# Top-k attention and Fourier mixing on one Trainium2 core: the scores of a pair's first tile queued last in TensorE's step

## The chip, the cores and the metric

The kernel runs on one core of a Trainium2 chip. The core has a TensorE for matmuls (PE in the profile; its weight loads are shown as PEld), a VectorE (DVE), a ScalarE (ACT), a GpSimd (POOL) and a SyncE (SP), which issues the DMAs here. Each engine works through its own list of instructions in order; the lists are tied together by semaphores. The metric is the device time of one execution in microseconds.

## The reference

Two stages follow one another. In the first, 8 batches of 8 heads attend over 576 tokens with 64 channels a head, and only the 32 largest scores of a row are kept. The second takes the heads side by side as 512 channels, adds the real part of a two-dimensional Fourier transform over tokens and channels, normalises, and applies an MLP of width 2048 with a residual.

```python
scores = scale * np.matmul(q, k.transpose(0, 1, 3, 2))
kth = np.partition(scores, -top_k, axis=-1)[..., -top_k:-top_k + 1]
scores = np.where(scores >= kth, scores, -1000000000.0)
attn = np.exp(scores - np.max(scores, axis=-1, keepdims=True))
attn = attn / (np.sum(attn, axis=-1, keepdims=True) + 1e-09)
x = np.matmul(attn, v)                  # heads are then put side by side: (8, 576, 512)
...
mixed = np.real(np.fft.fft(np.fft.fft(x, axis=1), axis=2)).astype(np.float32)
u = x + mixed
un = (u - np.mean(u, -1, keepdims=True)) / np.sqrt(var + 1e-06)
out = u + np.maximum(un @ w_ch1, 0.0) @ w_ch2
```

All inputs and outputs are float32.

## The kernel before

**Tiles and pairs.** Two heads of a batch make a *pair*; there are 32 pairs, four to a batch. The 576 rows of queries are cut into four tiles of 128 rows and one of 64. A pair is worked through as nine *items*, in the order of `IN_PAIR`: tile 0 for each head, tile 1 for each head, the 64-row tile for both heads at once, tile 2 and tile 3 for each head. So item 9p is pair p's first tile, first head.

**The steps.** The main loop runs one *step* for each item number i, and in a step all engines get work of several items, a few items apart, so that none waits for another:

- `scores(j, ...)` for item j = i + 3: TensorE multiplies the queries (qT) by the first 512 keys (kT) for both heads of the tile (L401, tiles `sp`), and by the 64 last keys of both (kt, L371, `sp_t`). ScalarE copies the results from PSUM to the tile S in SBUF (L404 and L375; for the 64-row tile L386 on TensorE and L393 on ScalarE).
- `top_ops`: VectorE finds the 32 largest of a row, eight at a time (L425, L427); it finishes item i and begins item i + 1.
- `bounds` (POOL, L434, tile `nt`), `mask` (ScalarE L448, then POOL's subtraction L451) and `expo` (ScalarE L459) turn the scores of item i - 1 into unnormalised probabilities P.
- P must be transposed for the product with v. In the first batch and in pairs 7 and 31 TensorE does this (`transposes`, L527 to L545). In the others, those for which `pair_by_dma` holds (pairs 4 to 30 without 7), it goes by DMA: ScalarE splits P into two planes of 16-bit words (`plane`, L472, item i - 2), a DMA writes them to DRAM (L485, L488), and a transposing DMA (`turn`, L506, item i - 3) reads them back as PT. All three are issued in SP's order.
- `attend` (TensorE L564) multiplies PT by v, and `to_tokens` (TensorE L604, tile `tpx`) brings the result back to token rows, which VectorE normalises (L608).
- `prep` transposes the q and k of the next pair on TensorE (L308, tiles `tpq`, `tpk`); ScalarE copies them to qT and kT (L316, L318) and to kt (L322). k's turn is in step 9p + 5, q's in step 9p.
- `some` fills TensorE with *units* of the MLP of the batch before: `hidden` (hp, L966; ScalarE applies the ReLU at L970), `back` (cp, L993 and L1032), and `fast` (cv, cw, cz, L1163, a product with seven instead of eight sub-products, whose sums POOL makes at L1108).
- Once in a batch the Fourier transform of the batch before stands in a few steps: POOL folds x (L651 to L719), TensorE transforms over tokens (`dft_tokens`, yp, L755), ScalarE copies y (L786 to L798), TensorE transforms over channels (`dft_channels`, mp, L812 and L816), ScalarE copies us (L833), POOL adds it to x (L839), and VectorE takes the statistics (L844).

**What sets the order.** The order on every engine is written out by the program: the loop body appends TensorE's work of a step to the list `fixed` and then calls the entries one after the other; a call records all instructions of that piece of work on all engines, so a piece's ScalarE copies stand in ScalarE's list where the piece was called. After each entry, `some` adds MLP units up to that entry's share of the room that the step has by the planner's costs (`step_us`, `fixed_cost`, `level`). Before the first entry the step records `turn`, `mask` of item i - 1 and `plane` of item i - 2. After the entry with number `n_mask` = 0 come pieces put off from earlier (`act`, `out_next`). After the last entry before the transposes comes `expo` of item i - 1; in the pairs by DMA that is the end of the list.

The scores of a tile are the first entry of `fixed`. For a tile whose two heads are separate items and whose pair goes by DMA, both parts are one entry, at the first head's step. For a pair's first tile this is step 9p - 3, that is the step right after the one in which `prep` made the kT of that pair.

Of the kernel before, what the change touches and what calls it, by code (L numbers as in the profile page):

```python
# [73 lines left out]
def kernel(  # L74
# [55 lines left out]
    def bank(shape, name, hold=False):  # L130
        n = banks_free.pop(0)
        t = ps_m.tile(shape, F32, name=name, tag=f"m{n}", bufs=1)
        if not hold:
            banks_free.append(n)
            return t
        return t, lambda: banks_free.append(n)
# [157 lines left out]
    def prep(n, pair, blocks=((0, NF), (NF, NC))):  # L294

        if pair >= NPAIR:
            return 0.0
        src, got_of = nat[n, pair], qT_of if n == "q" else kT_of
        if pair not in got_of:
            got_of[pair] = attp.tile(  # L300
                [P, S if n == "q" else NF * P], F32, name=f"{n}T_{pair}", tag=f"{n}T",
                bufs=2 if n == "q" else 1
            )
        t_sb = got_of[pair]
        for c0, c1 in blocks:
            tp = ps_t.tile([P, 4, P], F32, name=f"tp{n}_{pair}_{c0}", tag="tp")
            for c in range(c0, c1):
                nc.tensor.transpose(  # L308
                    tp[:, c - c0, :], src[:, c, :, :].rearrange("p h d -> p (h d)"), ident
                )  # L310
            if c0 < NF:
                dst, got = t_sb[:, c0 * P:c1 * P], tp.rearrange("p a c -> p (a c)")[:, 0:(c1 - c0) * P]
            else:
                dst, got = t_sb[:, NF * P:], tp[:, 0, 0:TAIL]
            if n == "q":
                nc.scalar.mul(out=dst, in_=got, mul=scale)  # L316
            elif c0 < NF:
                nc.scalar.copy(out=dst, in_=got)  # L318
            else:
                for e in range(2):  # L320
                    r = slice(D * e, D * (e + 1))
                    nc.scalar.copy(out=kt_t[r, TAIL * e:TAIL * (e + 1)], in_=tp[r, 0, 0:TAIL])  # L322
        return 0.7
# [3 lines left out]
    PER_PAIR = len(IN_PAIR)  # L327
    PER_BATCH = NPB * PER_PAIR
# [3 lines left out]
    N = len(items)  # L332

    def scores(i, part):

        if not 0 <= i < N:
            return 0.0
        pair, t, e = items[i]  # L340
        qT, kT = qT_of[pair], kT_of[pair]
        rows = ROWS[t]
        if part == 0:
            for n in range(1 if e is None else 2):
                Ssb[i + n] = attp.tile([P, S], F32, name=f"S_{i + n}", tag="S", bufs=6)
        q_cols = slice(P * t, P * t + rows)


        plain = (slice(0, NF * P), slice(NF * P, S))
        tails_first = (slice(TAIL, S), slice(0, TAIL))  # L350
        if e is None:
            to = [
                (Ssb[i], slice(TAIL * h, TAIL * (h + 1)), *(tails_first if h and by_dma(i) else plain))
                for h in range(2)
            ]
        else:
            to = [
                (Ssb[i], slice(0, P), *plain),
                (Ssb[i + 1], slice(0, P), *tails_first),
            ]  # L360
        if part == 1:

            copy = nc.scalar.copy if i else nc.vector.tensor_copy
            shape, name = [P, NF * P], f"sp_{i}_t"
            if by_dma(i):
                sp = ps_t.tile(shape, F32, name=name, tag="tp")
            else:
                sp = ps_s.tile(shape, F32, name=name, tag="sp") if i else bank(shape, name)

            q_end = P * t + rows  # L370
            nc.tensor.matmul(  # L371
                sp[:, 0:P], lhsT=qT[:, q_end - P:q_end], rhs=kt_t, start=True, stop=True
            )
            for h, (s_t, r, _, tails) in enumerate(to):
                copy(out=s_t[r, tails], in_=sp[P - rows:P, TAIL * h:TAIL * (h + 1)])  # L375
            return 0.3
        if e is None and i >= PER_BATCH:

            half = NF * P // 2
            sps = [  # L380
                ps_s.tile([P, NF * P], F32, name=f"sp_{i}_{h}", tag="sp") for h in range(2)
            ]
            for g in range(2):
                for h in range(2):
                    hd = slice(D * h, D * (h + 1))
                    nc.tensor.matmul(  # L386
                        sps[h][TAIL * g:TAIL * (g + 1), 0:half],
                        lhsT=qT[hd, q_cols], rhs=kT[hd, half * g:half * (g + 1)],
                        start=True, stop=True,
                    )  # L390
            for h, (s_t, r, keys, _) in enumerate(to):
                for g in range(2):
                    nc.scalar.copy(  # L393
                        out=s_t[r, keys][:, half * g:half * (g + 1)],
                        in_=sps[h][TAIL * g:TAIL * (g + 1), 0:half],
                    )
            return 0.6
        for h, (s_t, r, keys, _) in enumerate(to):
            hd = slice(D * h, D * (h + 1))
            sp = ps_s.tile([P, NF * P], F32, name=f"sp_{i}_{h}", tag="sp")  # L400
            nc.tensor.matmul(  # L401
                sp[r], lhsT=qT[hd, q_cols], rhs=kT[hd, :], start=True, stop=True
            )
            nc.scalar.copy(out=s_t[r, keys], in_=sp[r])  # L404
        return 1.04
# [32 lines left out]
    def pair_by_dma(pair):  # L438

        return NPB <= pair < NPAIR - 1 and pair != 2 * NPB - 1  # L440

    def by_dma(i):
        return pair_by_dma(i // PER_PAIR)
# [999 lines left out]
    def chunk_at(i):  # L1443

        for tile in (i - 4, i - 3, i - 2):
            r = tile % PER_PAIR
            if PER_BATCH <= tile < N and r in (4, 8):
                if i - tile == (4 if by_dma(tile) else 2 if tile == 2 * PER_BATCH - 1 else 3):
                    return tile // PER_PAIR, r // 8
        return None, None  # L1450

    def fixed_cost(i):

        t = 0.55 if 0 <= i - 2 < N and not by_dma(i - 2) else 0.0
        if i + 3 < N:
            t += {0: 1.04, 1: 0.3, None: 0.9}[items[i + 3][2]]
            if by_dma(i + 3) and items[i + 3][2] is not None:
                t += -0.3 if items[i + 3][2] else 0.3
        ch = chunk_at(i)[1] if i > PER_BATCH + 3 else {4: 0, 8: 1}.get((i - 3) % PER_PAIR)
        t += 0.0 if ch is None else (CW[ch] / 115.0 + 0.14 * len(CHUNKS[ch]))  # L1460
        if i < N and i % PER_PAIR in (0, 5):
            t += 0.7
        return t + costs.get(i, 0.0)

    def level(i):

        steps = range(i, next((a for a in arrivals if a > i), i + PER_BATCH))
        rest, lev = sum(u[0] for u in queue + waiting), 0.0
        while lev < 6.4 and sum(max(0.0, lev - fixed_cost(s)) for s in steps) < rest:
            lev += 0.02  # L1470
        return lev

    def run(i, where):
        for fn in plan.pop((i, where), []):
            fn()
# [16 lines left out]
    while i < N + 5 or plan or queue or sums:  # L1492
# [11 lines left out]
        fixed, j = [], i + 3  # L1504
        e = items[j][2] if j < N else None
# [4 lines left out]
            preps.append(lambda: prep("q", pair_of + 1))  # L1510
        if i < N and i % PER_PAIR == 5:
            preps.append(lambda: prep("k", pair_of + 1))
        if e == 0 and by_dma(j):
            fixed.append(lambda: scores(j, 0) + scores(j, 1))
        elif e != 1:
            fixed.append(lambda: scores(j, 0))
        elif not by_dma(j):
            fixed.append(lambda: scores(j - 1, 1))
        else:
            fixed.append(lambda: 0.0)  # L1520
# [30 lines left out]
        if i in arrivals:  # L1551
            carry = min(carry, 0.0) if i > arrivals[0] else -5.0
            run(i, "units")
            step_us = level(i)
        room = step_us - carry - fixed_cost(i)
        cost, got = carry, 0.0
        turn(i - 3)
# [105 lines left out]
```

## Time and profile before

| | |
|---|---|
| median of three runs | 1877.12 us (1875.2 to 1878.28) |
| the profiled execution, its own time | 1876.57 us |
| its span, first to last instruction | 1874.8 us |
| mean granted TensorE clock | 0.955 |
| costliest group on TensorE | hp L966, 529.5 us, 2048 matmuls |
| costliest group on VectorE | L425, 626.5 us, 864 instructions |
| scores on TensorE, L401 | 170.7 us, 528 matmuls |
| transposing DMAs, L506 | 130, issued by SP |

The profile is one execution. A timeline line has the start in us from the span's beginning, the duration, the engine, the source line, the operation, tiles as out<-in, shapes and the number of instructions merged into the line; in brackets stands how long the engine was idle before it, and what ended that. A line of waits has the waiting group, what it waited for, the total in us, how many times, and the longest. A line of windows has the stretch and its length, then for each engine the busy time and the number of instructions, then the granted TensorE clock (1.00 is full speed), the busy share of the DMA engines, and GB/s. The slices on the page cut the span into 40 equal parts and give the busy tenths of each.

In TensorE's lines a float32 matmul appears as two records, so the two 512-key products of a tile are four records of L401.

### The profile page before, as it was taken

Reading aid. Unit: us, or ns where it says so; the run is one execution under the profiler, and the core shown is the slowest. Engines: PE = TensorE matmul, PEld = TensorE weight load, DVE = VectorE, ACT = ScalarE, POOL = GpSimd, SP = SyncE. Lnnn points to the kernel's source line nnn. Section 1 sums busy time; section 2 is a strip of 40 time slices with the busy share of each in tenths; the row PEclk is TensorE's granted clock in tenths of the full one; section 3 lists DMA queues with packets and bytes.
Section 4 is the critical chain, followed back from the end, with each engine's and each line's share of the span. In section 5 each row is a group of like instructions: output and inputs, shape, how many; then the busy total and the mean of one; then the engine's idle time right before and its main releaser. Section 6 shows DMA issues by size and latency. Waiting matters only on the chain.

```text
span 1874.8 us, 26903 instructions
## 1 busy us (share of the span) xinstructions
PE 1703.8 (91%) x8134; PEld 1086.4 (58%) x8134; DVE 1583.8 (84%) x3301; ACT 1295.0 (69%) x3104; POOL 912.5 (49%) x1278
## 2 busy tenths in 40 slices
PE   5566699789899899999999999989999999999999
PEld 3344465355466555666556565666567555677677
DVE  7999989888899999999999899899999899762110
ACT  6878659577788788877787678767787678652100
POOL 4768643454746266355545465255545364341012
PEclk7777799999999999999999999999999999999999
DMA  5333016661557755586466745694566645530132
GB/s 167 104 98 109 20 46 170 168 164 26 137 146 202 187 130 136 150 209 161 123 161 180 180 114 132 155 231 127 122 162 182 172 121 143 130 111 6 51 114 69
DMA packets 516576, 249.16 MB, mean 133 GB/s; under 512 B 398288, under 2 KB 506448, under 8 KB 516432
## 3 DMA queue, kind: packets, MB, share of 16 engines
q1 hardware_dynamic: 515664, 247.23, 50.9%
q8 instruction: 65, 1.06, 0.2%
q14 instruction: 79, 0.65, 0.1%
q10 hardware_dynamic: 768, 0.21, 0.0%
HBM read 93.63 MB, written 84.74 MB: 95 GB/s over the span
## 4 chain that ended last, share of the span: by engine, by line
PE 55%; DVE 13%; ACT 10%; POOL 10%; issue 6%; DMA 4%; SPq 2%; POOLq 0%; DVEq 0%; ACTq 0%
PE hp L966 22%; PE o L564 7%; DVE wk L427 6%; DVE m L425 6%; PE sp L401 4%; PE cp L993 4%; POOL wk L451 4%; PE cw L1163 3%; PE cv L1163 3%; PE cp L1032 3%; ACT wk L448 2%; POOL fg L651 2%; PE yp L755 2%; ACT wk L472 2%; PE sp_t L371 2%
## 5 line engine op out<-in xcount | busy, mean ns | idle before, releaser
L451 POOL TENSOR_TENSOR wk<-S,wk 128x576 f32<-128x576 f32 x288 | 408.1, 1417 | 549.8 <-ACT wk L448 533.9
L425 DVE MAX8 m<-wk 128x8 f32<-128x576 f32 x864 | 626.5, 749 | 6.2
L966 PE MATMUL hp<-unT,w 128*128 128x256 f32 (+1 forms) x2048 | 529.5, 411 | 5.2 <-ACT unT L884 2.7
L966 PEld LDWEIGHTS hp<-unT,w 128*128 128x128 f32 x2048 | 382.5, 192 | 116.5 <-issue 10.7
L427 DVE MATCH_REPLACE8 wk<-m,wk 128x576 f32<-128x576 f32 x576 | 427.4, 742 | 0.0
L472 ACT COPY wk<-S 128x576 uint16<-128x576 uint16 x468 | 289.1, 668 | 0.0
L448 ACT ACTIVATE wk<-S,nt 128x576 f32<-128x576 f32 x288 | 222.9, 774 | 85.4 <-POOL nt L434 84.5
L564 PE MATMUL o<-PT,v 128*64 128x256 f32 (+3 forms) x1440 | 204.8, 430 | 37.9 <-DMA PT<-planes 19.5
L993 PE MATMUL cp<-w,hT 128*128 128x512 f32 x512 | 236.4, 602 | 0.0
L425 DVE MAX8 m<-S 128x8 f32<-128x576 f32 x288 | 213.5, 741 | 7.8 <-ACT S L375 7.8
L459 ACT ACTIVATE S<-wk,nt 128x576 f32<-128x576 f32 x234 | 184.2, 787 | 48.3 <-POOL wk L451 47.2
L427 DVE MATCH_REPLACE8 wk<-m,S 128x576 f32<-128x576 f32 x288 | 213.5, 741 | 0.0
L970 ACT ACTIVATE hT<-hp 128x320 f32<-128x320 f32 (+1 forms) x256 | 103.9, 412 | 156.3 <-PE hp L966 155.2
L401 PE MATMUL sp<-kT,qT 64*128 64x512 f32 (+1 forms) x528 | 170.7, 676 | 24.2 <-ACT kT L318 9.4
L564 PEld LDWEIGHTS o<-PT,v 128*64 128x64 f32 x1440 | 117.9, 158 | 114.9 <-issue 37.0
L404 ACT COPY S<-sp 128x512 f32<-128x512 f32 (+1 forms) x264 | 141.6, 586 | 24.4 <-PE sp L401 23.3
L993 PEld LDWEIGHTS cp<-w,hT 128*128 128x128 f32 x512 | 93.4, 193 | 91.4 <-issue 91.0
L1108 POOL TENSOR_TENSOR hT<-hT 128x512 f32<-128x512 f32 x64 | 81.6, 1277 | 106.5 <-ACT hT L970 91.5
L434 POOL TENSOR_TENSOR nt<-m,cc 128x2 f32<-128x2 f32 x288 | 59.1, 205 | 126.2 <-DVE m L425 122.5
L371 PEld LDWEIGHTS sp_t<-kt,qT 128*128 128x128 f32 x320 | 51.3, 196 | 108.9 <-issue 70.0
L1163 PE MATMUL cw<-w,hT 128*128 128x256 f32 x448 | 105.0, 381 | 1.5 <-POOL hT L1108 0.9
L527 PE MATMUL tpP<-ident,wk 128*128 128x128 f32 x216 | 40.8, 320 | 61.1 <-ACT wk L459 36.1
(160 smaller groups left out, 2174.3 us busy)
## 6 DMA issues: line engine op xcount, KB each, us to landing
planes<-wk SPq DMA_DIRECT2D x208, 288.0 KB, 2.7
w<-w_parts SPq DMA_DIRECT2D x82, 512.0 KB, 4.7
space<-in_moe_w_ch_dram SPq DMA_DIRECT2D x32, 512.0 KB, 3.7
nat<-in_q_dram SPq DMA_DIRECT2D x128, 64.0 KB, 2.7
v<-in_v_dram SPq DMA_DIRECT2D x64, 128.0 KB, 3.0
out_dram<-x SPq DMA_DIRECT2D x32, 256.0 KB, 2.7
nat<-in_k_dram SPq DMA_DIRECT2D x62, 128.0 KB, 3.0
planes<-wk SPq DMA_DIRECT2D x52, 144.0 KB, 2.6
```

The costliest lines, as they stand in the source:

```text
L401: nc.tensor.matmul(sp[r], lhsT=qT[hd, q_cols], rhs=kT[hd, :], start=True, stop=True)
L404: nc.scalar.copy(out=s_t[r, keys], in_=sp[r])
L425: ops.append(lambda src=src, m8=m8: nc.vector.max(out=m8, in_=src))
L427: ops.append(lambda src=src, m8=m8: nc.vector.match_replace(w, m8, src, NEG))
L448: nc.scalar.activation(out=w, in_=Ssb[i], func=AF.Relu, scale=-FAR, bias=Nt[i][:, 1:2])
L451: nc.gpsimd.tensor_tensor(out=w, in0=Ssb[i], in1=w, op=ALU.subtract)
L459: nc.scalar.activation(out=Ssb[i] if by_dma(i) else w, in_=w, func=AF.Exp, bias=Nt.pop(i)[:, 0:1], accum_out=den_t[pair % 3][:, c:c + 1],)
L472: nc.scalar.copy(out=words[:, half, :], in_=src[:, half, :])
L564: nc.tensor.matmul(o[D * e:D * (e + 1), c0:c1], lhsT=vv[:, c, e, :], rhs=pt[:, NF if c == NF else (NF + 1) * e + c, c0:c1], start=(c == 0) ...
L966: nc.tensor.matmul(hp[:, 0:w], lhsT=w1[:, dt, P * it:P * (it + 1)], rhs=unT[:, dt, 0:w], start=(dt == 0), stop=(dt == NDT - 1),)
L993: nc.tensor.matmul(cp, lhsT=hT[:, it, P * n:P * (n + 1)], rhs=w2[:, it, :], start=(it == 0), stop=(it == NIT - 1),)
L1163: nc.tensor.matmul(dst, lhsT=h()[a][:, kc, :], rhs=rhs_of(kc), start=start and kc == 0, stop=kc == NK - 1, skip_group_check=True,)
```

## The change

In the pairs whose P goes by DMA, except pair 4 (whose first item is number `PER_BATCH`), the scores of a pair's first tile are no longer the first entry of `fixed` but are appended as its last one. An entry that does nothing takes the first place, so that what is recorded after entry 0 keeps its place. The condition `j % PER_PAIR == 0` picks the first item of a pair; it holds for pairs 5, 6 and 8 to 30, which are 25 pairs. Everything else in the step is the same, and so is the list of units; how many units stand before the scores follows from the share of room that `some` gives each entry.

```diff
-        if e == 0 and by_dma(j):
+        last_scores = []
+        if PER_BATCH < j < N and j % PER_PAIR == 0 and by_dma(j):
+            fixed.append(lambda: 0.0)
+            last_scores.append(lambda: scores(j, 0) + scores(j, 1))
+        elif e == 0 and by_dma(j):
             fixed.append(lambda: scores(j, 0) + scores(j, 1))
         elif e != 1:
             fixed.append(lambda: scores(j, 0))
...
             run(i, "units")
             step_us = level(i)
+        fixed += last_scores
         room = step_us - carry - fixed_cost(i)
         cost, got = carry, 0.0
         turn(i - 3)
```

In the built program TensorE's and ScalarE's lists change, and those of VectorE, POOL and SP do not. In 19 of the 25 pairs the six records of scores move behind one MLP unit, in some of them behind a `tpx` or the transposes as well; in the six pairs 9, 14, 18, 22, 26 and 30 they move behind the 42 records of the token transform yp. ScalarE's copies of S move with them: behind the y copies in these six pairs, behind one ReLU or one scaled copy in most of the others.

## The prediction

> **What bounds the kernel now.** I read the page's busy shares and slices first, then busy time by batch, the waits, and at last the rows around the moved block in single pairs. Pairs are numbered from 0; a step handles one tile of a pair.
>
> The page, busy time and slices:
> ```profile
> PE 1703.8 (91%) x8134; PEld 1086.4 (58%) x8134; DVE 1583.8 (84%) x3301; ACT 1295.0 (69%) x3104; POOL 912.5 (49%) x1278
> ...
> PE   5566699789899899999999999989999999999999
> ...
> DVE  7999989888899999999999899899999899762110
> ```
> After the first seventh, TensorE and VectorE are both nearly full until about 1690 us; then TensorE alone finishes the last MLP. Busy time in two batches in the middle (PE, PEld, DVE, ACT, POOL, granted clock):
> ```profile
> 880.00:1090.00 210.00, 204.03 (x983) 129.38 (x984) 196.96 (x408) 162.13 (x388) 109.40 (x160) 0.98 0.63 159
> 1090.00:1300.00 210.00, 201.35 (x967) 126.49 (x966) 192.27 (x400) 157.84 (x377) 105.08 (x156) 0.98 0.61 155
> ```
> TensorE is at 96 to 97%, VectorE at 92 to 94%. Who waits for whom says which leads:
> ```profile
> DVE x L608 <- PE tpx L604: 57.3, 23, 6.7
> ...
> PE sp L401 <- ACT kT L318: 9.4, 8, 2.5
> ```
> VectorE waits for TensorE (57.3 us), so a microsecond taken from TensorE's chain is worth up to a microsecond, unless it meets a place where TensorE itself waits. The second row is the one the change touches: scores that wait for ScalarE's copy of kT. By pair, the gap before the first scores is 0.46 (pair 0), 2.46 (7), 1.41 (9), 0.48 (14), 1.16 (18), 1.15 (22), 1.16 (26), 1.15 (30). Pairs 0 and 7 keep their place; the six others, 6.51 us, are moved. In the other 19 moved pairs no gap stands before the scores. Pair 22, TensorE:
> ```profile
> 1130.61 1.88 PE L993 MATMUL cp<-w,hT 128*128 128x512 f32 x4
> 1133.63 1.13 PE L401 MATMUL sp<-kT,qT 64*128 64x512 f32 x4 [1.15 <-ACT kT L318]
> 1134.69 0.49 PE L371 MATMUL sp_t<-kt,qT 128*128 128x128 f32 x2
> 1135.11 0.72 PE L755 MATMUL yp<-fs,fg 128*64 128x145 f32 x8
> ...
> 1148.37 1.03 PE L564 MATMUL o<-PT,v 128*64 128x320 f32 x6
> ```
> and ScalarE:
> ```profile
> 1133.01 0.58 ACT L318 COPY kT<-tpk 128x512 f32<-128x512 f32 x1
> ...
> 1136.63 1.07 ACT L404 COPY S<-sp 128x512 f32<-128x512 f32 x2
> 1137.59 0.35 ACT L375 COPY S<-sp_t 128x64 f32<-128x64 f32 x2
> ...
> 1139.38 0.42 ACT L786 COPY y<-yp 128x288 f32<-128x288 f32 x1 [0.57 <-PE yp L755]
> ...
> 1140.60 0.77 ACT L459 ACTIVATE S<-wk,nt 128x576 f32<-128x576 f32 x1
> ```
> TensorE is free at 1132.49, kT is there at 1133.58, and behind the scores stands the token DFT (yp), which needs neither kT nor qT. The chain of waits runs through just this place: kT copy, scores, yp, y copy, mp, and TensorE without a pause to 1155.02.
>
> **The change part by part.** The instruction lists of the two programs differ on TensorE and ScalarE alone; VectorE, POOL and SP have the same instructions in the same order, so no DMA moves and nothing is added. In 25 pairs a block of 1.55 us (sp 1.13 and sp_t 0.49 overlapping, 1133.63 to 1135.18) moves behind what follows it, and its four copies move on ScalarE.
>
> *Nineteen pairs without a kT wait, 0.* The block goes behind one MLP unit (hp 2.35, cw or cp 1.9 us), in some with a tpx. TensorE does the same work in another order. What it could cost is lateness: S is late by up to 1.9 us. In pair 28 the copies end at 1445.9 and VectorE first reads that S at 1452.53, so 6.6 us cover it. The exponential (L459) stands behind these copies. In pairs where one ReLU (L970, 0.39) merely changes sides it is about 0.4 late and the next mask is not; in pair 28 it is 1 us late, and ScalarE has a 0.70 wait for TensorE right behind it. Without that cover the next mask, POOL's subtraction (L451, 1.41) and the masked tile's way out would be late by the remaining 0.3 to 1 us. One of the 19 is special: in pair 8 the four copies leave the place ahead of mask and exponential, and TensorE's 0.81 wait at 435.56 ends with that exponential. Ends: 0 and -0.8; two shorter waits on the same row follow at 450 and 453, so I take half, -0.4.
>
> *Pairs 22, 26, 30: -1.1, -0.8, -0.4.* POOL finished the folds at 1131.02, so yp can start at 1132.5 instead of 1135.11; the scores then run from 1136.7 and find kT done. TensorE is 1.1 us ahead. ScalarE: the y copies start at 1136.63 and follow yp closely, the S copies come at about 1138.8, the exponential at about 1140.0 instead of 1140.60, since the 0.57 wait goes. All that follows TensorE at mp moves with it. What is late next is the transposed P for attend (L564), whose DMA hangs on SP's queue and not on the scores: it landed at 1146.74 in pair 22 (attend at 1148.37), at 1357.26 in pair 26 (1358.04), at 1563.31 in pair 30 (1563.67). So 1.1, 0.78 and 0.36 get through. Behind attend, ScalarE's waiting copy of us and VectorE's next wait for tpx (6.02 at 1187.25) let it pass.
>
> *Pair 18: 0.* There P landed at 942.22 and attend began at 942.26 after a wait of 0.13: the gain waits at that place. Ends: 0, and -1.16 if the DMA lands as fast as in pair 22 (3.4 us from issue, against 4.1).
>
> *Pair 14: 0.* The chain of waits runs on VectorE from 714 to 755, without a gap. Ends: 0 and -0.48.
>
> *Pair 9: +0.6.* Here the folds are not ahead:
> ```profile
> 475.17 1.88 PE L993 MATMUL cp<-w,hT 128*128 128x512 f32 x4
> 478.46 1.13 PE L401 MATMUL sp<-kT,qT 64*128 64x512 f32 x4 [1.41 <-ACT kT L318]
> ...
> 480.24 0.46 PE L755 MATMUL yp<-fs,fg 128*64 128x145 f32 x2 [0.23 <-POOL fg L651]
> 481.51 0.59 PE L755 MATMUL yp<-fs,fg 128*64 128x145 f32 x5 [0.81 <-POOL fg L665]
> ```
> Now the scores fill part of a time that POOL sets; moved, they leave TensorE idle from 477.05 to 480.24 and come after yp. TensorE loses 1.55, which attend's wait of 3.19 at 492.11 covers; ScalarE stays busy either way and its exponential comes 0 to 0.3 later, which the POOL chain behind it feels. The bounds are 0 and, if yp also runs slower, 1.5; I take 0.6, nearer the small end, for this reason: TensorE's clock. The trace shows the granted clock falling after waits:
> ```profile
> 1154.00:1161.00 7.00, 4.54 (x34) 2.98 (x32) 6.83 (x18) 5.58 (x12) 3.23 (x5) 0.98 0.61 146
> 1161.00:1168.00 7.00, 7.00 (x15) 3.17 (x14) 6.93 (x16) 5.34 (x15) 4.28 (x16) 0.53 0.61 164
> ```
> A wait of 2.09 us at 1160.32 left TensorE at 0.53 for the next 7 us (some 3.4 us of work). It fell too after the 3.19 at 492.11 (0.59 over the next stretch), and did not after 2.84 at 841.44. Pair 9's 3.19 of new idle lies on that edge: 3.4 us at half clock would stretch yp by 1.7, of which about 1.5 could reach the exponential.
>
> [...]
>
> **Sum.** -0.4 -1.1 -0.8 -0.4 + 0.6 = -2.1. I allow +0.6 for the small late exponentials of the pairs like 28 (13, 20 and 28, 0.2 each, between 0 and the 0.3 left over): -1.5. The profiled execution took 1876.57 us around its span of 1874.8, so 1875.07; the median shown, 1877.12, is 0.55 above it: 1875.6.
>
> **The rivals.**
> *All waits come through.* If P lands earlier, too, or the waits at attend are not met, pairs 14 to 30 give 0.48 + 1.16 + 1.15 + 1.16 + 1.15 = 5.10, pair 8 gives 0.81, and pair 9 costs nothing: -5.9, 1871.2. For it: the chain of waits passes through kT in pairs 18 to 30. Against it: the landing times above.
> *The DFT's tail makes ScalarE late (slower).* If yp starts no earlier than now (as POOL makes it in pair 9; a PSUM bank held by a unit would do the same), scores come only after 1139.35, their copies end near 1142.0 and the exponential comes 1.3 late; then mask, POOL's L451, and nt, behind which POOL adds us and VectorE already waits (2.70 at 1145.16). TensorE loses its 1.15 wait again elsewhere. Five pairs at 1.3 are 6.5, with pair 9's 1.5 about +8: 1885; half of it, 1881, if covers hold. It decides from the point where yp starts later than 1133.8 in pair 22's terms. Against it: folds done at 1131.02, 1.5 us before TensorE is free.
> *All gains are swallowed* at attend and at scores that wait for ScalarE's S copies (L393: 2.09 at 1160.32, 1.73 at 751.19): 0, 1877.1.
>
> **How the numbers follow.** My sum has 0.42, all waits through 0.24, slower 0.20, swallowed 0.14. 0.2% is 3.75 us, about what a measurement of this kernel can tell from no change. Of the first case, 0.06 falls beyond -3.75 and 0.03 beyond +3.75 (clock phases: each half-clock stretch is worth 1.7 to 3.4 us, and four more or fewer are possible); all waits through is faster in 0.22 of its 0.24; the slower case counts fully but for 0.02. Faster 0.28, same 0.51, slower 0.21. My likeliest case alone spans 1872.5 to 1879; the range for 8 in 10 goes from 1869.5, beyond all waits through by one half-clock stretch, to 1883.0, into the slower case.
>
> **What would show it.** Right: the wait of scores for kT falls from 9.4 to about 2.9 in total (pairs 0 and 7); in pairs 22, 26 and 30 yp starts within 0.1 us of the unit before it, the 0.57 wait of the y copy is gone, and attend waits for P in pairs 18, 26 and 30; in pair 9 a wait of yp for POOL of about 3.2. Wrong: yp waits for something else in pairs 14 to 30, VectorE waits for S, the wait at L844 grows, or new half-clock stretches appear near 927, 1343 or 481.

## The result, and the profile after

| | before | after |
|---|---|---|
| median of eleven runs | 1877.12 us | 1873.54 us |
| ratio, with its 95% interval | | 0.9969 (0.9960 to 0.9979) |
| profiled execution, own time | 1876.57 us | 1868.68 us |
| its span | 1874.8 us | 1866.9 us |

The ratio stands for -5.8 us (0.31%), the two medians for -3.6; single executions of the same kernel lie up to 10 us apart, which the last section explains in part. The interval of the ratio ends below 1, so the change made the kernel faster.

The page of the changed kernel: TensorE and VectorE have the same busy time as before (1704.1 against 1703.8, 1584.9 against 1583.8). Only waiting went.

```profile
PE 1704.1 (91%) x8134; PEld 1086.8 (58%) x8134; DVE 1584.9 (85%) x3301; ACT 1294.6 (69%) x3104; POOL 912.8 (49%) x1278
...
L425 DVE MAX8 m<-S 128x8 f32<-128x576 f32 x288 | 213.8, 742 | 16.1 <-ACT S L375 16.1
...
L401 PE MATMUL sp<-kT,qT 64*128 64x512 f32 (+1 forms) x528 | 169.0, 670 | 15.5 <-ACT S L393 7.7
```

The waits of the changed kernel (waiting group, what it waited for, total, times, longest):

```profile
DVE x L608 <- PE tpx L604: 52.1, 22, 7.9
...
DVE m L425 <- ACT S L375: 16.1, 9, 4.0
PE sp L401 <- ACT S L393: 7.7, 7, 2.1
...
PE sp L401 <- ACT kT L318: 1.3, 2, 0.9
...
DVE st L844 <- POOL x L839: 1.3, 4, 0.3
```

The two VectorE rows that moved most, in the kernel before:

```profile
DVE st L844 <- POOL x L839: 11.0, 8, 2.7
...
DVE m L425 <- ACT S L375: 7.8, 3, 4.0
```

The scores' wait for kT fell from 9.4 to 1.3 us, and what is left is pairs 0 and 7. Of this fall 6.5 is the moved pairs; the rest is pair 7, which keeps its place and waited 2.46 in this profile of the kernel before, 0.99 in a second one and 0.86 here. VectorE's wait for TensorE fell by 5.2, but two profiles of the kernel before differ by as much (57.3 and 62.9), so this row tells nothing. Two rows changed places: the wait at L844 fell from 11.0 to 1.3, and VectorE's wait for S rose from 7.8 to 16.1. That second one was named beforehand as a sign of being wrong; experiment 4 is about what it costs.

Pair 22 of the changed kernel, first TensorE, then ScalarE (start, duration, instruction, and in brackets the idle time ahead of it):

```profile
1129.60 2.74 PE L993 MATMUL cp<-w,hT 128*128 128x512 f32 x6
1132.27 0.72 PE L755 MATMUL yp<-fs,fg 128*64 128x145 f32 x8
...
1136.42 1.13 PE L401 MATMUL sp<-kT,qT 64*128 64x512 f32 x4
1137.48 0.49 PE L371 MATMUL sp_t<-kt,qT 128*128 128x128 f32 x2
1137.81 0.61 PE L812 MATMUL mp<-fd,y 128*128 128x128 f32 x4
...
1146.75 1.57 PE L564 MATMUL o<-PT,v 128*64 128x320 f32 x10
```

```profile
1132.87 0.57 ACT L318 COPY kT<-tpk 128x512 f32<-128x512 f32 x1
...
1136.49 0.43 ACT L786 COPY y<-yp 128x288 f32<-128x288 f32 x1
...
1138.57 1.06 ACT L404 COPY S<-sp 128x512 f32<-128x512 f32 x2
1139.53 0.34 ACT L375 COPY S<-sp_t 128x64 f32<-128x64 f32 x2
1139.73 0.80 ACT L459 ACTIVATE S<-wk,nt 128x576 f32<-128x576 f32 x1
```

yp starts with no pause, the scores find kT there, the y copies run without the 0.57 wait, and the exponential stands 6.86 us behind the start of the kT copy, against 7.59 before (1140.60 - 1133.01). Attend stands 13.88 behind it, against 15.36. From the kT copy to attend this is 1.5 us shorter.

To see where the rest went I measured each profile from the start of one pair's kT copy to that of the next, and added the pairs up by stage. Kernels that share a trait (pair 9 moved or not, and so on) can then be set side by side; the columns not yet introduced are experiments of the next section (five, six and rest are numbers 1, 6 and 2, again is a second profile of the same kernel). A stretch in which the granted clock is 0.50 is called a half-clock stretch.

| us | before | again | five | six | rest | after | again |
|---|---|---|---|---|---|---|---|
| pairs 5 to 7 | 152.4 | 152.1 | 152.3 | 152.5 | 151.4 | 152.0 | 152.2 |
| pair 8 | 50.6 | 50.6 | 50.6 | **48.1** | **48.1** | **48.1** | **48.1** |
| pairs 9 to 13 | 247.7 | 246.2 | 246.0 | 246.8 | **249.1** | **248.4** | **252.1** |
| pairs 18 to 30 | 673.9 | 677.9 | **669.7** | **670.6** | 673.3 | **666.3** | **669.7** |

In bold: pair 8 moved; pairs 9 to 13 moved, all five of them; pairs 18, 22, 26 and 30 moved. Pair 8 gives 2.5 us in every one of these profiles. Pairs 9 to 13 lose 3.2 (mean of the bold ones 249.9, of the others 246.7). Pairs 18 to 30 give 6.0 (675.1 to 669.1). The sum is -5.3; the timed ratio says -5.8. Pairs 14 to 17, left out of the table, take 203.0 on average in the profiles with pair 14 in its place (201.2 to 204.8) and 203.3 in those with it moved. Each column is one execution, so the rows tell where time went and the ratios tell how much.

### The profile page after: what moved, and what is told of

Same layout as the page of the kernel before. It is cut to its first block, busy times and chain, and to the rows that moved or that the text cites. A ratio compares the mean times of both kernels' runs of the same rounds, so it can differ in the third digit from the quotient of the medians.

```text
span 1866.9 us, 26900 instructions
## 1 busy us (share of the span) xinstructions
PE 1704.1 (91%) x8134; PEld 1086.8 (58%) x8134; DVE 1584.9 (85%) x3301; ACT 1294.6 (69%) x3104; POOL 912.8 (49%) x1278
## 4 chain that ended last, share of the span: by engine, by line
PE 61%; DVE 14%; POOL 7%; ACT 7%; DMA 4%; issue 4%; SPq 1%; POOLq 0%; DVEq 0%
PE hp L966 22%; PE cp L993 8%; PE o L564 7%; DVE m L425 6%; DVE wk L427 6%; PE sp L401 4%; PE cw L1163 4%; PE yp L755 3%; POOL wk L451 3%; PE cv L1163 3%; PE cp L1032 2%; PE sp_t L371 2%; ACT wk L448 1%; DMA PT<-planes 1%; DMA planes<-wk 1%
## 5 line engine op out<-in xcount | busy, mean ns | idle before, releaser
L564 PE MATMUL o<-PT,v 128*64 128x256 f32 (+3 forms) x1440 | 209.3, 437 | 34.7 <-DMA PT<-planes 18.6
L425 DVE MAX8 m<-S 128x8 f32<-128x576 f32 x288 | 213.8, 742 | 16.1 <-ACT S L375 16.1
L401 PE MATMUL sp<-kT,qT 64*128 64x512 f32 (+1 forms) x528 | 169.0, 670 | 15.5 <-ACT S L393 7.7
L371 PEld LDWEIGHTS sp_t<-kt,qT 128*128 128x128 f32 x320 | 50.6, 193 | 108.5 <-issue 69.8
```

The source lines that it names most:

```text
L401: nc.tensor.matmul(sp[r], lhsT=qT[hd, q_cols], rhs=kT[hd, :], start=True, stop=True)
L425: ops.append(lambda src=src, m8=m8: nc.vector.max(out=m8, in_=src))
L564: nc.tensor.matmul(o[D * e:D * (e + 1), c0:c1], lhsT=vv[:, c, e, :], rhs=pt[:, NF if c == NF else (NF + 1) * e + c, c0:c1], start=(c == 0) ...
```

## The experiments

**1. Only the five pairs whose scores waited for kT behind an early yp.**

```diff
-        if PER_BATCH < j < N and j % PER_PAIR == 0 and by_dma(j):
+        if j < N and j % PER_PAIR == 0 and j // PER_PAIR in (14, 18, 22, 26, 30):
```

> Only pairs 14, 18, 22, 26 and 30 (scores behind yp) are moved; the other twenty keep their place. Theory A, the kT wait of these pairs is all of the gain: -4.5 us against the kernel before (1.5 each in 22, 26 and 30 and a little in 14 and 18, as the two traces show between the kT copies of neighbouring pairs), ratio 0.9976. Theory B, what the prediction said, the wait for P at attend takes most of it back: -2.3, ratio 0.9988. Theory C, the gain came from pairs 8 and 9 and the early stage: 0 to -1. In all of them the wait of scores for kT keeps the 2.46 of pair 7 and the 1.41 of pair 9 and loses the rest.

Measured: 0.9991 (0.9976 to 1.0006), profiled 1870.16. The timing alone decides nothing: theory A's 0.9976 lies on the edge of the interval, those of B and C inside it, and the profiled execution was the fastest of its twelve (median 1873.96). The profile is plain where no half-clock stretch interferes: pair 26 takes 45.53 us against 47.08 and pair 18 46.75 against 47.27, as in the changed kernel (45.51 and 46.80).

**2. The complement: all the others.**

```diff
-        if PER_BATCH < j < N and j % PER_PAIR == 0 and by_dma(j):
+        if PER_BATCH < j < N and j % PER_PAIR == 0 and by_dma(j) and j // PER_PAIR not in (14, 18, 22, 26, 30):
```

> The complement: twenty pairs are moved, 14, 18, 22, 26 and 30 keep their place. Theory A: -0.5 to -1.5, ratio 0.9995 (pair 8's 0.81 wait alone). Theory B: +0.5. Theory C: -4 to -5, ratio 0.9975. If the parts add up, this and the run with the five give the whole, 0.9969.

Measured: 1.0001 (0.9983 to 1.0018), profiled 1873.42. Pairs 22 and 26 are back at 51.63 and 47.07, with the waits of before (1.15 for kT, 2.7 at L844). Pair 8 keeps its gain of 2.5, and pairs 9 to 13 spend it. The expectation asked whether the parts add up: five and rest together come to 0.9992, give or take some 0.0023, where the whole gives 0.9969. By the timing they do so only at the very edge of the noise, and experiment 6 asks again.

**3. The kT wait removed in another way: k prepared one step earlier, scores first as before.**

```diff
-        if i < N and i % PER_PAIR == 5:
+        if i < N and i % PER_PAIR == (4 if pair_of + 1 in (14, 18, 22, 26, 30) else 5):
```

> The kernel before, with the scores in their old place, and instead the transposes and copies of the next k one step earlier for pairs 14, 18, 22, 26 and 30. If the wait for kT itself is the cost (theory A), taking it away in this other way gives the same as moving the scores, -3.5 to -4.5, ratio 0.998. If the order on ScalarE (y copies ahead of S copies, the 0.57 wait for yp gone) is what gives the gain, this kernel gains 1 us or less. The gap before the first scores of the five pairs is 0 in both.

Measured: 1.0015 (1.0001 to 1.0028), profiled 1881.26. No kT wait is left in the five pairs, and nothing is gained. TensorE of this kernel shows one reason, a step ahead of pair 26:

```profile
1337.00 1.88 PE L993 MATMUL cp<-w,hT 128*128 128x512 f32 x4
1338.72 0.60 PE L308 MATMUL tpk<-ident,nat 128*128 128x128 f32 x4
1340.18 0.33 PE L308 MATMUL tpk<-ident,nat 128*128 128x128 f32 x1 [0.86 <-ACT S L375]
```

The transposes of k now wait 0.86 for ScalarE's copy of the last tile's S; in pairs 18, 22 and 30 it is 0.85 to 0.88. And the wait at L844 stayed:

```profile
PE tpk L308 <- ACT S L375: 10.5, 5, 7.0
DVE st L844 <- POOL x L839: 9.7, 10, 2.6
```

(before: 3.6 and 11.0.) So the kT wait was not paid to the kT alone: ScalarE was late, and moving k only chose another place for TensorE to meet that. The whole time of this kernel is not the measure of it, for a second thing happened in pair 14: there the transposes of k waited 3.63 before and wait 7.04 now, and pairs 13 and 14 together take 106.0 us against 100.5. From the kT copy of pair 17 to that of pair 31, which holds the four other pairs, it takes 724.6 us against 725.0 and 729.1 in two profiles of the kernel before, and 717.4 and 720.8 in two of the changed kernel. The first two, 724.6 and 725.0, have equally much half clock (20.5 us). So in these four pairs, too, next to nothing is gained, which is what the second of the two theories said. This run doesn't separate the two causes cleanly, since an MLP unit also moved with the costs of the step. What it does show is that ending this wait is not enough to have the gain of the change.

**4. The scores between the two halves of yp.**

```diff
-        for where in ("pe1", "pe2", "pe"):
+        for where in ("pe1", "pe1b", "pe2", "pe"):
+            if where == "pe1b" and (i, where) in plan:
+                fixed += last_scores
+                last_scores = []
```

(with the two halves of `dft_tokens` planned as two entries, in batches 1 to 6.)

> As the changed kernel, but in the pairs with yp the scores stand between the two halves of yp instead of behind both. kT is still covered (half of yp takes 2.4 us, the wait was 1.15), and S is ready some 1.8 us earlier. If VectorE's new wait for S (1.8 us in pairs 22, 26 and 30) costs time, this kernel is 1 to 4 us faster than the changed one, ratio to the kernel before 0.995 to 0.9965. If that wait only takes the place of VectorE's old wait for POOL at L844, the time is that of the changed kernel, 0.9969, and the L844 wait is back at 1 to 2.7.

Measured: 0.9988 (0.9974 to 1.0002), profiled 1868.73. Both expectations are outside this interval, if only just: the kernel is slower than either said. In pair 26 one can follow VectorE's new wait. Against the changed kernel, the wait for S falls by 1.23 us, from 1.81 to 0.58; but mp then waits 0.78 for the y copies, L844 waits 1.31 again, and attend stands 14.65 behind the kT copy instead of 13.79. Pair 26 gives 0.70 instead of 1.57. VectorE's waits for S and at L844 together (0.58 + 1.31 + 0.32) are no shorter than with the scores behind all of yp (1.81 + 0.32), while before there was 2.70 + 0.32. So the wait for S takes the other's place rather than being added to it.

**5. The kernel before and the changed kernel once more, on one chip.**

> The kernel before, once more, against itself; it tells the noise of the comparison and gives a second profile of the half-clock stretches. Both theories: ratio 1.0000, with an interval that shows what a ratio of 0.9990 is worth. Theory of the waits (TensorE's wait for kT in the DFT pairs and the wait in pair 8 are the gain): pair 26 takes 47.08 us from kT copy to kT copy and pair 18 47.27 again, since no half-clock stretch lies in them; attend starts 15.36 behind the kT copy in pairs 22, 26 and 30. Theory of the clock (most of the gain of the changed kernel's profile is where the half-clock stretches fell): pair 22, 51.65 in the profile of before, comes out at 48.2 without a stretch behind the 2.09 wait, at 49.9 with one of 3.4 us, at 51.6 with one of 6.8.

> The changed kernel once more, on one chip with the others. Theory of the waits: pairs 18, 22, 26 and 30 are again 0.5, 1.2, 1.5 and about 1.0 shorter than before once half-clock stretches are set equal, pair 8 at least 0.8, together about 5; ratio 0.997 (0.9955 to 0.9985). Theory of the clock: the mechanism gives about 3, the rest of the difference of the two profiles was luck, and the ratio is 0.9985 or nearer to 1; pair 8 comes back to 49.8 or 50.6.

Measured: 1.0008 (0.9995 to 1.0020) for the kernel before against itself, and 0.9969 (0.9955 to 0.9982) for the changed one: the first result again, closer than the intervals would lead one to expect. The profiles are told in the table above. Pairs 18 and 26 of the kernel before repeat (47.37 and 47.09 us), pair 8 stayed at 48.13 in the changed kernel, and the ratio was not nearer to 1, so the theory that the difference of the profiles was luck falls there. Pair 22 of the kernel before decides nothing: it came out at 51.85 with again 6.8 us at half clock, as both theories have it. Luck holds for a part: pair 22 took 47.04, 48.78 and 49.61 us in three profiles with moved scores, with 0, 3.4 and 6.8 us at half clock behind the same 2.09 wait.

**6. Only six pairs: 8, 14, 18, 22, 26 and 30.**

```diff
-        if PER_BATCH < j < N and j % PER_PAIR == 0 and by_dma(j):
+        if j < N and j % PER_PAIR == 0 and j // PER_PAIR in (8, 14, 18, 22, 26, 30):
```

> Only the scores of pairs 8, 14, 18, 22, 26 and 30 queued last, nothing else. Theory of the waits: all that the change gives is in these pairs, so as fast as the changed kernel, ratio 0.997; pair 8 takes 48.1 (50.6 in before), with the 0.81 wait of the P transposes for the exponential gone. Theory of the other pairs (the 19 moves without a kT wait cost or give something of their own): six differs from the changed kernel by over 2 us, faster if they cost (pairs 11 to 13, 15, 16), slower if they give (pairs 5, 24).

Measured: 0.9970 (0.9956 to 0.9984), the same as the whole change. Six of the 25 moves carry all of it; the other 19, pair 9 among them, add up to nothing that the timing tells. This does not fit well with the 3.2 us that pairs 9 to 13 lose in the profiles: if every execution lost them and nothing else of the 19 gave anything, six should have come out at about 0.9952, just outside its interval. Either the loss is smaller on average than in three profiles, or other moves give some of it back; the runs leave that open.

**7. Every two-headed tile, not the pair's first alone.**

```diff
-        if PER_BATCH < j < N and j % PER_PAIR == 0 and by_dma(j):
+        if PER_BATCH < j < N and e == 0 and by_dma(j):
```

> From the second batch on, the scores of every two-headed tile of the pairs whose P goes by DMA are queued last, not those of a pair's first tile alone; no work is left out. The other tiles never wait for kT. Theory of the waits: nothing more to gain, 0 to 1 us slower than the changed kernel (ratio 0.997 to 0.998), since more S copies come late and VectorE's wait for S (16.1 us in the changed kernel) grows. Theory of order (TensorE's step as such runs better with the scores last, because what ScalarE needs first comes first): another 2 to 4 us faster, ratio 0.995.

Measured: 0.9927 (0.9912 to 0.9942), median 1864.17: 13 us faster than before and clearly faster than the change. My theory of the waits, which had nothing left to gain, was wrong. TensorE's wait for S L393 (8.3 us before) was down to 0.3, so the next experiments ask which tile did it.

**8. Tile 5 (the first one behind the 64-row tile) as well; tile 5 alone; tiles 2 and 7 alone.** The condition on the item is all that differs:

```diff
+        if PER_BATCH < j < N and j % PER_PAIR in (0, 5) and by_dma(j):
...
+        if PER_BATCH < j < N and j % PER_PAIR == 5 and by_dma(j):
...
+        if PER_BATCH < j < N and j % PER_PAIR in (2, 7) and by_dma(j):
```

> The changed kernel, with the scores of tile 5 (the first behind the four-row-block tile that both heads share) queued last as well; tiles 2 and 7 stay where they were. Theory of the narrow copies (scores of tile 5 come right behind those of tile 4, whose PSUM banks ScalarE empties in four narrow copies, L393; queued last they find the banks free): as fast as all four tiles last, ratio 0.9925 to 0.994; the wait of scores for S L393 falls from 8 to under 1 us, and the time of the L401 rows outside of waits, half-clock stretches taken out, falls from 127.5 to about 120. Theory of order (every tile gains a little): about half of the way, ratio 0.995.

> The kernel before, with the scores of tile 5 alone queued last in the pairs whose P goes by DMA, the pair's first tile as in before. Theory of the narrow copies: the gains add up, so 0.9927 / 0.9969 = 0.9958 of before, 1869.5; TensorE's wait for kT stays at 9 us and VectorE's wait at L844 at 11. Theory of order: 0.998 to 0.999. It also tells whether the kT waits are worth the same with tile 5 out of the way.

> The kernel before, with the scores of tiles 2 and 7 queued last, those of tiles 0 and 5 as in before. Theory of the narrow copies: no wait is taken away, ratio 1.000 to 1.001. Theory of order: 0.997 to 0.998, as all four are worth 0.9927 and the first alone 0.9969.

Measured: 0.9945 (0.9926 to 0.9964), 0.9976 (0.9962 to 0.9989) and 1.0006 (0.9994 to 1.0018). Tile 5 is a second gain that adds to the first (0.9969 x 0.9976 = 0.9945), tiles 2 and 7 give nothing by themselves. Tile 5 of pair 22, in the kernel before, and in the kernel with tiles 0 and 5 last:

```profile
1157.84 0.39 PE L371 MATMUL sp_t<-kt,qT 128*128 128x128 f32 x2
1160.32 2.84 PE L401 MATMUL sp<-kT,qT 64*128 64x512 f32 x4 [2.09 <-ACT S L393]
```

```profile
1158.86 0.39 PE L371 MATMUL sp_t<-kt,qT 128*128 128x128 f32 x2
1159.09 1.88 PE L993 MATMUL cp<-w,hT 128*128 128x512 f32 x4
1162.59 0.63 PE L881 MATMUL tpu<-ident,x 128*128 128x128 f32 x4 [1.62 <-POOL t L864]
1163.05 1.88 PE L993 MATMUL cp<-w,hT 128*128 128x512 f32 x4
1164.86 1.13 PE L401 MATMUL sp<-kT,qT 64*128 64x512 f32 x4
```

In the first, the scores come straight behind the tail scores of the 64-row tile, whose results ScalarE still has to take out of PSUM in four copies. They wait 2.09, and fall into a half-clock stretch (0.50 from 1160.69 on, 2.84 for the four records). In the second they stand behind MLP units and take 1.13 with no wait. There is a smaller form of it that no wait shows: in pair 25 of the kernel before, the four records take

```profile
1320.28 1.67 PE L401 MATMUL sp<-kT,qT 64*128 64x512 f32 x4
```

instead of 1.13, since the two heads' products, which otherwise run at the same time, start one after the other: at 1320.28 and at 1320.81, right behind the last of the four copies, which ends at 1320.78. In the kernel with tiles 0 and 5 last both start at 1164.86. The page's row of L401 has both, for the kernel with tiles 0 and 5 last:

```profile
L401 PE MATMUL sp<-kT,qT 64*128 64x512 f32 (+1 forms) x528 | 162.4, 674 | 6.9 <-ACT means L1351 2.9
```

Idle time 24.2 to 6.9, busy time 170.7 to 162.4. Of these 25 us the timing shows 10.3 (0.55%): a part meets new waits, such as the 1.62 for POOL in the rows above. By size, tile 5 alone speaks against my theory of the narrow copies (0.9958 lies outside 0.9962 to 0.9989) and fits the theory of order (0.998). What speaks against the theory of order is the run with tiles 2 and 7, where it asked for 0.997 to 0.998. So the place was right, and the share that comes through was not foreseen. One thing that may have eaten into it is visible: in the kernel with tile 5 alone, VectorE's wait at L844 grew to 14.1, where 11 was expected. That all four tiles (0.9927) beat tiles 0 and 5 (0.9945) isn't settled, as the intervals overlap.

## Why the prediction came out as it did

The direction and the range held (1871.3 by the ratio, 1873.54 by the median, in 1869.5 to 1883.0), but the likeliest case, -1.5 and too small to be told from no change, was not what happened. By size it was the rival "all waits come through" (-5.9), though not by its terms; that its total came so near is luck.

| term | predicted | measured, kT copy to kT copy |
|---|---|---|
| pair 8 | -0.4 | -2.5 (48.1 against 50.6, five profiles against four, in kernels that move no other tile) |
| pair 22 | -1.1 | -2.1 at equal half-clock stretches (49.61 and 49.69 against 51.65, 51.85 and 51.63) |
| pair 26 | -0.8 | -1.55 (45.5 against 47.1, in every profile) |
| pair 30 | -0.4 | -0.2 to -1.3 at equal stretches (52.63 to 53.75 against 53.94); two profiles with the scores first and less half clock took 52.3 and 52.4 |
| pair 18 | 0 | -0.6 (46.6 to 46.8 against 47.3 to 47.4) |
| pair 14 | 0 | 0 to +0.9 |
| pair 9 | +0.6 | 52.55, 52.87 and 57.14 against 51.84 to 52.76 |
| pairs 9 to 13 together | +0.6, and +0.2 for 13 | +3.2 |
| exponentials of 20 and 28 | +0.4 of the +0.6 | nothing that shows (pair 28: 56.65 and 56.81 against 56.83 and 57.54) |

*Right.* What moves where; that yp could start at once (1132.27) and that the 0.57 wait goes; that P at attend limits pair 18 (a wait of 1.21 at 942.03, where 0.13 stood) and in part pair 30 (0.18 in one profile of the changed kernel, 1.55 in the other); that pair 9 would leave TensorE waiting 3.17 us for POOL, and that the granted clock might fall there (it was 0.50 from 478.55 on, for 3.41 us):

```profile
477.93 0.46 PE L755 MATMUL yp<-fs,fg 128*64 128x145 f32 x2 [3.17 <-POOL fg L651]
```

The rival in which ScalarE gets late was rejected for the right reason: yp did not wait in pairs 14 to 30. Two of the signs did not come as written: attend did not wait for P in pair 26, and VectorE did wait for S.

*The step that failed in pair 26, and in part in pair 30: "What is late next is the transposed P for attend, whose DMA hangs on SP's queue and not on the scores: it landed at ...".* I took the landing times as fixed. In pair 26 P landed 14.56 to 14.63 behind the kT copy in the profiles with the scores first, and 13.2 to 13.7 in those with the scores last: it came 0.9 to 1.4 earlier, ahead of attend's new start at 13.8, so nothing was held back. In SP's queue the loads of the next q ahead of it took 3.18 us before and 2.16 after:

```profile
1343.48 3.18 SPq L240 DMA_DIRECT2D nat<-in_q_dram  x4
...
1347.76 2.60 SPq L506 DMA_TRANSPOSE PT<-planes  x1
...
1353.70 1.31 SPq L506 DMA_TRANSPOSE PT<-planes  x1
```

```profile
1337.48 2.16 SPq L240 DMA_DIRECT2D nat<-in_q_dram  x4
...
1340.72 2.45 SPq L506 DMA_TRANSPOSE PT<-planes  x1
...
1346.52 1.30 SPq L506 DMA_TRANSPOSE PT<-planes  x1
```

One of the four loads took 1.39 to 1.49 to issue in the three profiles with the scores first, and 0.47 in the four with them last. Why it does so stays open. In pair 30 P did not keep its time either: it landed 13.9 and 15.3 behind the kT copy in two profiles of the changed kernel, where 15.0 stood before, and attend came 1.3 earlier in one and 0.1 later in the other. In pair 22, where nothing was to be held back by my numbers, attend gained 1.5 rather than 1.1: L812, the first part of mp, starts 1.2 earlier behind the kT copy, and L816, the second, which needs a later y copy, starts 0.44 behind it instead of 0.67. Pair 22 as a whole gained 2.1; what the other 0.6 is was not found.

*The term of pair 8 was mis-sized.* The 0.81 wait went as described, and the two shorter waits behind it (0.43 and 1.84) stayed, as I had assumed. What I left out is the clock. The stretches around the 1.84 wait, in the kernel before and the changed one (length, busy times, then granted clock):

```profile
450.70:454.10 3.40, 1.55 (x10) 1.04 (x12) 3.37 (x7) 3.32 (x10) 2.71 (x8) 1.00 0.01 2
454.10:457.50 3.40, 3.40 (x19) 2.68 (x14) 2.33 (x5) 0.59 (x2) 0.22 (x2) 0.51 0.00 0
```

```profile
451.20:454.60 3.40, 2.01 (x16) 1.73 (x18) 3.37 (x8) 2.81 (x9) 2.52 (x9) 1.00 0.01 2
454.60:458.00 3.40, 3.40 (x17) 1.64 (x14) 2.29 (x6) 2.39 (x6) 1.17 (x1) 1.00 0.00 0
```

Coming 0.8 us earlier, the same wait no longer falls whole into one window of the clock (0.50 and 1.34 in two windows, where 1.84 lay in one; the last section has these windows), and the half clock behind it (3.41 us at 0.50, so by estimate worth 1.7 of the 2.5) is gone. That part is a matter of where the windows lie, not of the move as such: in the kernels of experiment 8 in which tile 5 is moved, pair 8 takes 49.6 us with its scores last and 49.3 with them first.

*The terms of pairs 9 to 13 were mis-sized the other way.* My +0.6 for pair 9 is not far from what it did in two of the three profiles in the table (52.55 and 52.87 against 51.84 to 52.76); in the third it took 57.14, with three half-clock stretches of 6.8 us. Half clock did set in at yp (at 478.6 in the changed kernel's first profile, one of the places named). The rest of the 3.2 comes at different places in different profiles, and since the scores of all five pairs are moved in these kernels, it can't be put down to pair 9. The piece that all of them share stands in pair 13, which takes 52.5 to 53.6 us against 51.0 to 51.1. There attend waits 2.63 and 2.59 for VectorE in the two profiles of the changed kernel, and 1.43 to 2.23 in the four with the scores first. The kernel before, and the changed one:

```profile
688.32 2.11 PE L564 MATMUL o<-PT,v 128*64 128x320 f32 x14 [1.80 <-DVE m L425]
```

```profile
684.16 4.54 PE L564 MATMUL o<-PT,v 128*64 128x320 f32 x16 [2.63 <-DVE m L425]
```

Half clock stands beside it (0.50 from 683.4 on, for 6.8 us), and attend takes 4.54 for 16 records where 14 took 2.11. TensorE arrives early, waits for VectorE all the same, and pays for the longer wait. I had put pair 13 at +0.2, for a late exponential.

*What I missed.* VectorE's wait for the moved S (1.81 in pairs 22, 26 and 30). I had costed the lateness of S from pair 28, with 6.6 us of cover; in the pairs of the Fourier transform there is none: in pair 22 VectorE was free for it at 1138.04, and S came at 1139.85. It seems to have done no harm because the 2.70 at L844, right behind it, went at the same time (experiment 4).

In the profiles the two errors, pair 8 and the limits on one side, pairs 9 to 13 on the other, partly cancel; the timing shows the first and not the second (experiment 6). The range held by 1.8 us at its lower end (1871.3 against 1869.5), and that it did is in part luck.

## What to carry to other kernels

A wait that a profile shows in front of an instruction can be just the place where a late engine is met: here bringing the input forward moved the wait (0.86 in place of 1.15) and gained next to nothing, while putting work without that input into the gap, which also gave the late engine its copies in a better order, gained about 1.5 us at attend in pairs 22 and 26. Don't hold the next limit fixed when you shift a step: check whether the work that feeds it comes out of the same queues. And when one such move pays, look for the same pattern elsewhere before tuning the first: the tile behind the four narrow copies was worth nearly as much (0.9976) as the change itself (0.9969), and all of them together 0.9927.

## What the runs showed of the hardware

**The half clock went by a grid of 3.41 us.** Within an execution the stretches at half clock begin at multiples of 3.413 us from one another, all 31 in the profile of the kernel before and all 33 in that of the changed one: before at 385.9, 454.1 and 491.7, for example, which are 20 and 11 such lengths apart. From 270 us on they last one or two of them in these two profiles (3.41 or 6.83 us), earlier up to three (10.24). I cut thirteen profiles into these windows (270 to 1690 us) and took TensorE's idle time in each window that ran at full clock. Of 4728 windows with less than 0.8 us idle none was followed by half clock, of 135 with 0.8 to 1.2 us 8 were, of 142 with 1.2 to 2.0 us 46, and of 138 with 2.0 us or more 137. In the two profiles named it was none of 729, 1 of 19, 5 of 22 and all of 22. So in these runs it wasn't the length of a wait that counted but how much idle time fell into one window: in the kernel before, attend's 2.84 wait ending at 841.44 lay in two windows, with 1.24 and 1.60, and no half clock followed; the 2.09 wait ending at 1160.32 lay whole in one, and the clock was 0.50 from 1160.69 on, for 6.83 us. The same wait in pair 22, cut by a window's end in both profiles of the changed kernel: in the second, with about 1.4 of it ahead of the half clock, and in the first, with 1.20 and 0.89 in two windows:

```profile
1154.50:1158.90 4.40, 2.62 (x24) 1.64 (x22) 4.37 (x12) 4.07 (x9) 2.35 (x2) 1.00 1.05 240
1158.90:1165.70 6.80, 6.13 (x10) 2.81 (x11) 6.59 (x17) 6.59 (x17) 4.51 (x19) 0.50 0.55 138
```

```profile
1151.00:1158.00 7.00, 5.25 (x37) 3.54 (x35) 6.90 (x17) 5.53 (x15) 3.16 (x4) 1.00 0.74 168
1158.00:1165.00 7.00, 6.30 (x20) 3.03 (x21) 6.79 (x17) 6.84 (x18) 4.75 (x19) 1.00 0.53 137
```

49.61 us for the pair with it, 47.04 without. That goes some way to explain why equal executions differ by several microseconds, and why a profile of each kernel can mislead by as much as the change is worth: the two profiled executions of the kernel before lie 6.5 us apart, those of the changed one 5.1.

**After the early part the program stood at one place of the grid.** At the kT copy of pair 0 the nine profiles whose order is the same up to pair 5 stand anywhere in the window (0.67 to 2.98 us into it); at the kT copy of pair 5 all nine stand at 1.60 to 1.69 (1.64 in the kernel before, 1.62 in the changed one). At pair 8 they still stand within 1.0 us of one another; by pair 14 they are spread over the window again (1.73 and 3.02 in those two). In the two kernels of experiment 8 with tile 5 moved, where pair 8's gain did not come, the kT copy of pair 5 stands at 3.23 and 3.26. This fits with pair 8's 2.5 us coming in every one of the nine profiles while pair 22's half clock came and went. That the waits and half-clock stretches of the first 270 us do the lining up is likely from this, but was not tested.
